# Attention with a squared-ReLU MLP on one core: the PV sums of a visit in a shared PSUM bank, copied by ScalarE and added up on GpSimd

## The chip, the cores and the metric

The kernel runs on one core of a Trainium2 chip. Its time is the device time of one execution in microseconds. All data are fp32; most matmuls read them as fp32r, and values that need more precision are split into a high and a low part that are multiplied apart.

## The reference

One layer norm feeds two branches. Branch A is attention with 32 heads of 16 columns over 2048 positions; branch B is a dense layer of 512 to 1792 with squared ReLU, a second dense layer back to 512, and SiLU. The output is `x + A * silu(B)`.

```python
xn = _layernorm(x)                                   # x: (1, 2048, 512)
q, k, v = split_heads(xn @ wqkv)                     # 32 heads of 16
p = softmax(einsum("bhqd,bhkd->bhqk", q, k) * 16 ** -0.5)
s = merge_heads(einsum("bhqk,bhkd->bhqd", p, v)) @ wo
h = relu(xn @ w1 + b1) ** 2                          # 512 -> 1792
g = silu(h @ w2 + b2)                                # 1792 -> 512
out = x + s * g
```

(`split_heads` and `merge_heads` stand for the reshapes and transposes of the reference.)

## The kernel before

**Units and steps.** Attention is cut into 32 units: four heads by 512 queries each. A unit has 16 steps, one for every 128 keys. A step has four matmuls of keys by queries, one a head, whose result goes through `exp` on ScalarE (`exp_mm`, matmul L1337, exp L1349), and the PV product of the four heads. In addition every step has four matmuls of queries by keys for a unit that is 24 steps ahead (`max_mm`, matmul L367); VectorE reduces each to the maximum over its 512 keys (L374). These maxima are the shift of the softmax: they come back into the query tiles as extra rows, so an exp needs no bias. We call the matmuls of L1337 and L367 the QK matmuls.

**Row tiles.** A QK matmul uses 64 rows of TensorE, so two matmuls run side by side in two lanes. The kernel fills the second lane with the dense layers of branch B, whose matmuls are cut into halves of 64 rows (L268 and L236). One round is what the two lanes start together: as a rule one QK matmul and one piece of dense work.

**Long slots.** `dense` yields the dense work in order, eight chunks of 256 positions. Where a piece has 12 units of work for each lane (`block`), `long_slots` spreads it over four steps: 28 rounds with 16 exps and 16 maxima. 24 rounds have dense work; the rounds in `DOUBLE` have a QK matmul in both lanes instead. The string in `ORDERS` says which QK matmul is an exp (`s`) and which a maximum (`m`). After 12, 16 and 28 rounds (`VISITS`) TensorE visits PV for 1, 1 and 2 steps. In the first dense layer a round has two matmuls of 256 columns, in the second one of 512. A chunk has 13 long slots; four of its steps, around the border between the two halves of its second layer, are single slots (`slot`), each with a PV visit of one step.

**PSUM.** There are eight banks. One (`pd`) holds the sums of the dense work. One (`pv`, tile `po`) holds the PV sums of a unit over all its 16 steps. Six hold results of QK matmuls: three are called `se`, three `pm_t`, but any of them may take an exp or a maximum. When the program is written out, a small model of TensorE's time picks the bank: `ROUND`, `FIRST_ROUND`, `STEP` and `VISIT` advance TensorE's clock, `READERS` and `READY` say when ScalarE or VectorE will have read a bank, and `flow_take` chooses one that is free by then. What happens on the chip is kept right by semaphores.

**PV.** `pv_mm` (L453) runs four matmuls, one a head, in four groups of 32 columns of TensorE, with `start` in the first step of a unit and `stop` in the last. After the last, `evac` copies the bank to the SBUF tile `ot` on ScalarE (L463). Then come, some steps apart, a DMA of the row sums (L473), their reciprocal on VectorE (L479), a DMA to DRAM and a broadcast back (L482, L488), the multiplication and a split on GpSimd (L502 to L504) and the stores (L511).

**The order of work.** TensorE, ScalarE, VectorE, GpSimd and SP's DMA queue each run their instructions in the order in which the program writes them. `later(n, fn)` writes `fn` out n steps later. GpSimd also squares and splits the first layer's result (L618, L109, L110) and adds the second layer's bias (L637), on which ScalarE's tanh waits (L642). Where one lane has finished its half of a dense block, a `fence` puts a `nop` on ScalarE that the other lane's first matmul waits for.

Three buffers `ex` in SBUF serve to load weights; that is over before unit 4.

Of the kernel before, what the change touches and what calls it, by code (L numbers as in the profile page):

```python
# [9 lines left out]
F32 = mybir.dt.float32  # L10
F32R = mybir.dt.float32r
AF = mybir.ActivationFunctionType
# [38 lines left out]
    [(0, 0), (0, 2), (1, 0), (1, 2), (2, 0), (2, 2)],  # L51
    [(0, 1), (0, 3), (1, 1), (1, 3), (2, 1), (2, 3)],
)
DOUBLE = (11, 13, 14, 27)
VISITS = {12: 1, 16: 1, 28: 2}
QUARTERS = (7, 14, 21, 28)
ORDERS = ("smsmsmsmsmssmmsmssmsmsmssmsmmmms", "smsmsmsmsmssmmsmssmsmsmssmsmmmms")
ROUND = 232
FIRST_ROUND = 335
STEP = 907  # L60
VISIT = 185
READY = 450
READERS = {"s": (476, 675), "m": (600, 745), "d": (600, 755)}
EPS = 1e-5


# [1 line left out]
def kernel(  # L68
# [56 lines left out]
    with ExitStack() as ph:  # L125
# [136 lines left out]
        def block(mms, per, post, between={}):  # L262


            def emit(ms, lane, follow):
                r = slice(64 * lane, 64 * lane + 64)
                for out_, lh, rh, first_, last_ in ms:
                    mm = nc.tensor.matmul(  # L268
                        out_, lh(r), rh(r),
                        start=first_ and lane == 0, stop=last_ and lane == 1,  # L270
                        skip_group_check=True,
                    )
# [12 lines left out]
            assert len(units) == 12  # L285
            yield [
                [
                    lambda m=m, lane=lane, k=k: [
                        emit(m, lane, None if k else last_use[0]),
                        lane and k in between and between[k](),  # L290
                    ][0]
                    for k, m in enumerate(units)
                ]
                for lane in range(2)
            ], post, ORDERS[per == 1]

        def terms3(ps, terms):

# [37 lines left out]
        def flow_visit(n):  # L336
            flow["pe"] += VISIT + n * STEP
            flow["fresh"] = True

        def flow_take(kind):  # L340
            free = [i for i, spot in enumerate(spots) if spot[0] <= flow["pe"] and spot[2] == kind]
            at, t, _ = spots.pop(min(free or range(len(spots)), key=lambda i: spots[i][0]))
            flow["pe"] = max(flow["pe"], at)
            return t

        def flow_give(t, kind):
            every, held = READERS[kind]
            begin_ = max(flow[kind], flow["pe"] + READY)
            flow[kind] = begin_ + every
            spots.append([begin_ + held, t, kind])  # L350

        def flow_bank(kind):
            t = flow_take(kind)
# [94 lines left out]
                        ),  # L448
                    )

        def pv_mm(po, qd, kb, pts):
            for j in range(4):
                nc.tensor.matmul(  # L453
                    po[32 * j : 32 * j + 32, :],
                    vs[qd][:, (4 * kb + j) * VW : (4 * kb + j) * VW + 32], pts[j],
                    start=(kb == 0), stop=(kb == NT - 1), skip_group_check=True,
                )

        def evac(po, u):
            qd, qc = divmod(u, 4)  # L460
            cs = slice(qc * 512, (qc + 1) * 512)
            ot = sp.tile([P, 512], F32, name="ot", bufs=1)
            nc.scalar.activation(ot, po, AF.Copy)  # L463
            if u == NU - 3:
                unit_mid(ot)
                return
            for n, fn in zip(EVAC, (evac_sums, evac_recip, evac_keep, evac_back, evac_norm, evac_store)):
                later(n, lambda fn=fn: fn(u, ev))
            ev = {"ot": ot}
# [1068 lines left out]
        def pv_step(st, pts):  # L1538
            u, kb = divmod(st, 16)
            if kb == 0:  # L1540
                pos[0] = pv.tile([P, 512], F32, name="po")
            pv_mm(pos[0], u // 4, kb, pts)
            if kb == NT - 1:
                if u < NU - 2:
                    evac(pos[0], u)
                elif u == NU - 2:
                    unit_inner(pos[0])
                else:
                    unit_final(pos[0])

        def dense():
            mp = ExitStack()
# [111 lines left out]
                post()  # L1664
            max_end(g)

        def long_slots(st0, units, post, order):

            if not spots:
                flow_start((pe, "se", "s", 3), (pm, "pm_t", "m", 3))  # L1670
            todo = [[(st0 + k, j) for k in range(4) for j in (lane, lane + 2)] for lane in range(2)]
            for kb in range(st0, st0 + 4):
                pts.setdefault(kb, {})
            ops, st, pv_at = list(order), st0, st0 - 2

            def fence(mm):
                use = nc.scalar.nop()
                tc.add_manual_dep(
                    use.ins, mm.ins.name,
                    mybir.DependencyInfo(  # L1680
                        mybir.DependencyClass.Sync, mybir.DependencyReason.DATA
                    ),
                    reason="the row tile is done with the bank",
                )
                last_use[0] = use

            def qk(lane):
                if ops.pop(0) == "m":
                    return max_mm(lane)
                kb, j = todo[lane].pop(0)  # L1690
                return exp_mm(kb, j, pts[kb], False)

            for r in range(len(order) - 4):
                if r in QUARTERS:
                    st += 1
                    begin(st)
                if r in DOUBLE:
                    for lane in range(2):
                        qk(lane)
                else:  # L1700
                    h = 0 if units[0] else 1
                    qk(1 - h)
                    mm = units[h].pop(0)()
                    if not units[h]:
                        if h and post is not None:
                            post()
                            last_use[0] = None
                        else:
                            fence(mm)
                flow_round()  # L1710
                if r + 1 in QUARTERS:
                    max_end(st + LEAD)
                    shift_due(st + 1 + LEAD)
                for _ in range(VISITS.get(r + 1, 0)):
                    pv_step(pv_at, pts.pop(pv_at))
                    pv_at += 1
                if r + 1 in VISITS:
                    flow_visit(VISITS[r + 1])
            assert not ops and not todo[0] and not todo[1] and not units[0] and not units[1]

        def plain_slot(st):
# [23 lines left out]
        for st_ in range(NU * 16):  # L1745
            if st_ < done:
                continue
            begin(st_)
            if st_ == FIRST:
                qs.close()  # L1750
            item = next(dn, None)
            if st_ == FIRST:

                for g in (LEAD, LEAD + 1):
                    max_end(g)
                for fn in last_store:
                    fn()
            if item is not None and len(item) > 2:
                assert st_ % 4 == 0
                long_slots(st_, *item)  # L1760
                done = st_ + 4
                to_visit[0] = st_ + 2
                continue
            wait = st_ >= LAST_MAX and item is not None and item[0] is not None and (st_ + flip[0]) % 2
            if item is not None and item[0] is not None:
                slot(st_, *item)
            else:

# [5 lines left out]
            for step in range(to_visit[0], st_ - 1):  # L1774
                pv_step(step, pts.pop(step))
            flow_visit(st_ - 1 - to_visit[0])
            to_visit[0] = st_ - 1
        assert not [1 for it in stream for _ in it] and not left
        run_waiting(True)
        assert not waiting and next(dn, None) is None  # L1780
        flow["on"] = False
        for st_ in range(to_visit[0], NU * 16):
            pv_step(st_, pts.pop(st_))
        wstk.close()


# [24 lines left out]
```

## Time and profile before

| What | us |
| --- | --- |
| median of three runs | 1616.87 |
| lowest and highest of the three | 1610.39 and 1617.13 |
| the profiled execution | 1610.35 |
| its span | 1608.6 |
| TensorE busy in the span | 1595.1 |
| VectorE busy | 1345.8 |
| ScalarE busy | 1189.6 |
| GpSimd busy | 534.9 |

In the rows of the profile PE is TensorE's matmuls, PEld its weight loads, DVE VectorE, ACT ScalarE and POOL GpSimd. A row of the timeline has the start in us from the start of the span, the duration in us, the engine, the line, the operation, the tiles written and read, their shapes, how many instructions are merged, and in brackets how long the engine sat idle before and what ended that. Matmuls overlap in the array and their ends are modelled, so the time between two starts says more than a duration. A row of a group has the sum and the mean (ns) of its instructions, then the idle time before them.

### The profile page before, as it was taken

To read this page: it belongs to the slowest core of one execution; us is meant where nothing else is said; L and a number is where in the kernel's file an instruction comes from. 1 tells how busy PE (TensorE), PEld (TensorE's weight loads), DVE (VectorE), ACT (ScalarE), POOL (GpSimd) and SP (SyncE) were. 2 spreads that over 40 slices of the span, in tenths; PEclk is the share of its full clock that TensorE was granted. 3 is DMA by queue.
4 is the path that set the end of the run, shared out by engine and by line. 5 is a ranking of instruction groups with operands and counts; after the bars stand their busy time and mean duration, and the time that the engine had idled before them with its cause. 6 is when DMAs were issued, how large, how long until landed. Compare 5 with 4: busy or idle time off the path is not lost.

```text
span 1608.6 us, 36225 instructions
## 1 busy us (share of the span) xinstructions
PE 1595.1 (99%) x13660; PEld 964.0 (60%) x13660; DVE 1345.8 (84%) x2307; ACT 1189.6 (74%) x2347; POOL 534.9 (33%) x610
## 2 busy tenths in 40 slices
PE   8999999999999999999999999999999999999998
PEld 7798665566546654665566456655665566545543
DVE  7486888888888888888888888888888888887764
ACT  7212777788778777887788778777877788778886
POOL 6436766233113311331133113311331134214621
PEclk9999999999999999999999999999999999999999
DMA  8977556435343433433434334433442253236755
GB/s 293 245 239 229 180 159 158 135 94 131 81 106 90 115 75 95 134 88 98 92 106 106 83 92 123 116 83 81 128 128 56 67 152 86 68 93 213 224 178 182
DMA packets 164174, 209.20 MB, mean 130 GB/s; under 512 B 59136, under 2 KB 79360, under 8 KB 162432
## 3 DMA queue, kind: packets, MB, share of 16 engines
q1 hardware_dynamic: 163856, 206.63, 46.4%
q8 instruction: 108, 1.77, 0.5%
q14 instruction: 66, 0.54, 0.1%
q10 hardware_dynamic: 144, 0.26, 0.0%
HBM read 148.90 MB, written 56.34 MB: 128 GB/s over the span
## 4 chain that ended last, share of the span: by engine, by line
PE 96%; DMA 1%; DVE 1%; issue 0%; SPq 0%; ACT 0%; POOL 0%; DVEq 0%
PE po L453 30%; PE pd_t L268 13%; PE pm_t L367 12%; PE se L1337 11%; PE se L367 8%; PE pm_t L1337 6%; PE pm_t L1206 4%; PE pd_t L236 4%; PE pm_t L236 2%; PE pd_t L1206 1%; PE se L1176 1%; PE se L1110 1%; PE pm_t L1297 0%; DVE mx L374 0%; PE se L236 0%
## 5 line engine op out<-in xcount | busy, mean ns | idle before, releaser
L374 DVE TENSOR_REDUCE mx<-pm_t 128x1 f32<-128x512 f32 x1236 | 799.2, 683 | 134.8 <-PE pd_t L268 82.4
L1349 ACT ACTIVATE pt<-se 128x512 f32<-128x512 f32 x1240 | 686.1, 606 | 182.8 <-PE pd_t L268 90.9
L374 DVE TENSOR_REDUCE mx<-se 128x1 f32<-128x512 f32 x795 | 528.5, 683 | 64.3 <-PE se L367 28.2
L1337 PE MATMUL se<-qe,ka 64*128 64x512 f32 x1346 | 530.4, 417 | 0.7 <-ACT pt L1349 0.7
L453 PE MATMUL po<-pt,v 128*32 128x512 f32 x3820 | 498.4, 602 | 0.2 <-DVE tsm L898 0.2
L367 PE MATMUL pm_t<-ka,qm 64*128 64x512 f32 x1236 | 480.4, 408 | 0.1
L1349 ACT ACTIVATE pt<-pm_t 128x512 f32<-128x512 f32 x666 | 388.9, 606 | 101.0 <-PE pd_t L268 58.5
L268 PE MATMUL pd_t<-xc,w1s 64*128 64x256 f32 x2352 | 328.8, 286 | 0.0
L1337 PEld LDWEIGHTS se<-qe,ka 64*128 64x128 f32 x1346 | 241.1, 184 | 137.1 <-ACT pt L1349 107.7
L367 PE MATMUL se<-ka,qm 64*128 64x512 f32 x795 | 310.6, 410 | 0.2
L268 PE MATMUL pd_t<-w2t,hT 64*128 64x512 f32 x1080 | 298.5, 408 | 0.0
L268 PEld LDWEIGHTS pd_t<-xc,w1s 64*128 64x128 f32 x2352 | 295.0, 186 | 0.0
L367 PEld LDWEIGHTS pm_t<-ka,qm 64*128 64x128 f32 x1236 | 222.9, 184 | 112.9 <-DVE mx L374 98.2
L1337 PE MATMUL pm_t<-qe,ka 64*128 64x512 f32 x695 | 283.6, 418 | 0.0
L453 PEld LDWEIGHTS po<-pt,v 128*32 128x32 f32 x3820 | 87.8, 108 | 158.7 <-issue 143.3
L268 PEld LDWEIGHTS pd_t<-w2t,hT 64*128 64x128 f32 x1080 | 180.9, 184 | 3.2
L367 PEld LDWEIGHTS se<-ka,qm 64*128 64x128 f32 x795 | 145.6, 184 | 51.5 <-DVE mx L374 36.0
L1337 PEld LDWEIGHTS pm_t<-qe,ka 64*128 64x128 f32 x695 | 126.3, 184 | 79.5 <-ACT pt L1349 64.4
L618 POOL TENSOR_TENSOR r<-r 128x512 f32<-128x512 f32 x56 | 58.2, 1039 | 321.1 <-ACT r L615 321.1
L502 POOL TENSOR_TENSOR ot<-ot,hl 128x512 f32<-128x512 f32 x27 | 34.7, 1286 | 154.5 <-DMA hl<-r_d 88.1
L637 POOL TENSOR_TENSOR u<-u,b_t 128x512 f32<-128x512 f32 x16 | 20.5, 1284 | 164.4 <-ACT u L636 164.4
L110 POOL TENSOR_TENSOR hT<-r,hT 128x512 fp32r<-128x512 f32 x56 | 72.5, 1295 | 4.7
(184 smaller groups left out, 1552.5 us busy)
## 6 DMA issues: line engine op xcount, KB each, us to landing
w1s<-w_d SPq DMA_DIRECT2D x196, 256.0 KB
qm<-q_d SPq DMA_DIRECT2D x384, 32.0 KB
ka<-k_d SPq DMA_DIRECT2D x96, 128.0 KB
qe<-q_d SPq DMA_DIRECT2D x384, 32.0 KB
q_d<-hl SPq DMA_DIRECT2D x16, 512.0 KB
g<-g_d SPq DMA_DIRECT2D x32, 256.0 KB
k_d<-hl SPq DMA_DIRECT2D x15, 512.0 KB
on_d<-hl SPq DMA_DIRECT2D x116, 64.0 KB
```

Of the source, the lines that this page charges most:

```text
L110: (lo or nc.gpsimd).tensor_tensor(dst[1], raw, dst[0].bitcast(F32), op=ALU.subtract)
L236: mm = nc.tensor.matmul(out_, lh(r), rh(r), start=first_ and lane == 0, stop=last_ and lane == 1, skip_group_check=True,)
L268: mm = nc.tensor.matmul(out_, lh(r), rh(r), start=first_ and lane == 0, stop=last_ and lane == 1, skip_group_check=True,)
L367: nc.tensor.matmul(ps, qms[u][p][64 * j : 64 * j + 64, qb * P : (qb + 1) * P], kas[qd, p][64 * j : 64 * j + 64, kc * 512 : (kc + 1) * 512] ...
L374: return nc.vector.tensor_reduce(mxs[u][:, c, kc : kc + 1], ps, axis=AX.X, op=ALU.max)
L453: nc.tensor.matmul(po[32 * j : 32 * j + 32, :], vs[qd][:, (4 * kb + j) * VW : (4 * kb + j) * VW + 32], pts[j], start=(kb == 0), stop=(kb = ...
L502: nc.gpsimd.tensor_tensor(ot, ot, rb, op=ALU.mult)
L618: nc.gpsimd.tensor_tensor(r, r, r, op=ALU.mult)
L637: nc.gpsimd.tensor_tensor(u, u, b2_t, op=ALU.add)
L1206: mm = nc.tensor.matmul(out_, lh(r), rh(r), start=first_ and lane == first, stop=last_ and lane != first, skip_group_check=True,)
L1337: nc.tensor.matmul(se, kas[qd, j // 2][b : b + 64, kb * P : (kb + 1) * P], qes[u][j // 2][b : b + 64, :], start=True, stop=True,)
L1349: return nc.scalar.activation(pts[j], se, AF.Exp, scale=0.25)
```

## The change

In units 4 to 27 a PV visit no longer adds to one bank over the whole unit. The bank `po` joins the six of the QK matmuls, seven in all, and each visit takes one of them, opens sums of its own in it and closes them at the visit's end. ScalarE copies them to SBUF: for the first visit of a unit into the unit's sum (`ot` in odd units, `ex0` in even ones), for the others into one of two part buffers (`ex1` and `ex2` in turn), which GpSimd adds to the sum. The steps after the last visit (`evac_chain`) are those of before, on that sum.

For long slots in these units the rounds with two QK matmuls move from 11, 13, 14 and 27 to 0, 13, 14 and 16, and there are two orders of exps and maxima, one for each dense layer. The numbers of the model that picks banks change for the whole kernel. In units 0 to 3 and 28 to 31 PV keeps its own bank.

```diff
-DOUBLE = (11, 13, 14, 27)
+DOUBLE = ((11, 13, 14, 27), (0, 13, 14, 16))
-ORDERS = ("smsmsmsmsmssmmsmssmsmsmssmsmmmms", "smsmsmsmsmssmmsmssmsmsmssmsmmmms")
+ORDERS = (
+    ("smsmsmsmsmssmmsmssmsmsmssmsmmmms",) * 2,
+    ("smmssmsmsmmssmmsmsssmsmmsssmsmmm", "msmsssmmssmsmmsmssmsmmsssmsmmmms"),
+)
+PARTS = range(4, 28)
-STEP = 907
-VISIT = 185
+STEP = 858
+VISIT = 226
-READERS = {"s": (476, 675), "m": (600, 745), "d": (600, 755)}
+READERS = {"s": (476, 785), "m": (600, 855), "d": (600, 865)}
+VISIT_READY = 160
...
         def flow_give(t, kind):
-            begin_ = max(flow[kind], flow["pe"] + READY)
+            begin_ = max(flow[kind], flow["pe"] + READY + (FIRST_ROUND - ROUND if flow["fresh"] else 0))
...
+        def flow_part(t):
+            begin_ = max(flow["s"], flow["pe"] + VISIT_READY)
+            flow["s"] = begin_ + READERS["s"][0]
+            spots.append([begin_ + READERS["s"][1], t, "s"])
...
-                    start=(kb == 0), stop=(kb == NT - 1), skip_group_check=True,
+                    start=first, stop=last, skip_group_check=True,
...
         def pv_step(st, pts):
             if kb == 0:
+                if u - 1 in PARTS:
+                    spots[:] = [spot for spot in spots if spot[1] is not pos["shared"]]
                 pos[0] = pv.tile([P, 512], F32, name="po")
-            pv_mm(pos[0], u // 4, kb, pts)
+            pv_mm(pos[0], u // 4, kb, pts, kb == 0, kb == NT - 1)
...
+        def pv_visit(st, n):
+            u, kb = divmod(st, 16)
+            if u not in PARTS:
+                for k in range(n):
+                    pv_step(st + k, pts.pop(st + k))
+                flow_visit(n)
+                return
+            if "shared" not in pos:
+                pos["shared"] = pv.tile([P, 512], F32, name="po")
+                spots.append([flow["pe"], pos["shared"], "s"])
+            po = flow_take("s")
+            for k in range(n):
+                pv_mm(po, u // 4, kb + k, pts.pop(st + k), k == 0, k == n - 1)
+            flow_visit(n)
+            if kb == 0:
+                if u % 2:
+                    pos["sum"] = sp.tile([P, 512], F32, name="ot", bufs=1)
+                else:
+                    pos["sum"] = rot["ex"][0]
+                nc.scalar.activation(pos["sum"], po, AF.Copy)
+            else:
+                rot["ex"][1:] = rot["ex"][:0:-1]
+                part = rot["ex"][1]
+                nc.scalar.activation(part, po, AF.Copy)
+                nc.gpsimd.tensor_tensor(pos["sum"], pos["sum"], part, op=ALU.add)
+            flow_part(po)
+            if kb + n == NT:
+                evac_chain(pos["sum"], u)
```

All places that ran `pv_step` over a visit's steps call `pv_visit` instead, and `long_slots` picks `DOUBLE` and `ORDERS` by whether its slot starts in one of these units.

More of the change, by code (lines that the diff above doesn't have):

```diff
@@ L294, in block @@
                 for lane in range(2)
-            ], post, ORDERS[per == 1]
+            ], post, per == 1
         def terms3(ps, terms):
@@ L449, in shift_rows, with pv_mm @@
                     )
-        def pv_mm(po, qd, kb, pts):
+        def pv_mm(po, qd, kb, pts, first, last):
             for j in range(4):
@@ L463, in evac, with evac_chain @@
             nc.scalar.activation(ot, po, AF.Copy)
+            evac_chain(ot, u)
+        def evac_chain(ot, u):
             if u == NU - 3:
@@ L1665, in slot, with long_slots @@
             max_end(g)
-        def long_slots(st0, units, post, order):
+        def long_slots(st0, units, post, second):
             if not spots:
@@ L1673, in long_slots @@
                 pts.setdefault(kb, {})
+            parts = st0 // 16 in PARTS
+            double, order = DOUBLE[parts], ORDERS[parts][second]
             ops, st, pv_at = list(order), st0, st0 - 2
@@ L1696, in long_slots @@
                     begin(st)
-                if r in DOUBLE:
+                if r in double:
                     for lane in range(2):
@@ L1713, in long_slots @@
                     shift_due(st + 1 + LEAD)
-                for _ in range(VISITS.get(r + 1, 0)):
-                    pv_step(pv_at, pts.pop(pv_at))
-                    pv_at += 1
                 if r + 1 in VISITS:
-                    flow_visit(VISITS[r + 1])
+                    pv_visit(pv_at, VISITS[r + 1])
+                    pv_at += VISITS[r + 1]
             assert not ops and not todo[0] and not todo[1] and not units[0] and not units[1]
@@ L1773 @@
                 continue
-            for step in range(to_visit[0], st_ - 1):
-                pv_step(step, pts.pop(step))
-            flow_visit(st_ - 1 - to_visit[0])
+            pv_visit(to_visit[0], st_ - 1 - to_visit[0])
             to_visit[0] = st_ - 1
@@ L1782 @@
         for st_ in range(to_visit[0], NU * 16):
-            pv_step(st_, pts.pop(st_))
+            pv_visit(st_, 1)
         wstk.close()
```

## Prediction

> **What bounds the kernel now.** I read the page's busy times first, then the timeline of TensorE over one long slot of each dense layer, then the weight loads that waited there, then ScalarE's and VectorE's own rows.
>
> ```profile
> PE 1595.1 (99%) x13660; PEld 964.0 (60%) x13660; DVE 1345.8 (84%) x2307; ACT 1189.6 (74%) x2347; POOL 534.9 (33%) x610
> 349.01:1435.22 1086.21, 1085.52 (x9589) 631.85 (x9589) 959.25 (x1609) 848.49 (x1684) 278.30 (x311) 1.00 0.39 99
> ```
>
> The second row is the window view from the evacuation of unit 3 to that of unit 27, 1086.2 us, where the change acts (columns: PE, PEld, DVE, ACT, POOL busy, clock, DMA). TensorE is busy throughout at full clock, so its small waits must be looked for inside the slots. A long slot is 28 rounds in segments of 12, 4 and 12, each followed by a PV visit. One whose dense work is the second layer, TensorE alone:
>
> ```profile
> 591.06 0.49 PE L1337 MATMUL pm_t<-qe,ka 64*128 64x512 f32 x1
> 591.39 0.39 PE L367 MATMUL se<-ka,qm 64*128 64x512 f32 x1
> ...
> 593.50 0.39 PE L1337 MATMUL se<-qe,ka 64*128 64x512 f32 x1
> ...
> 593.74 0.47 PE L1337 MATMUL pm_t<-qe,ka 64*128 64x512 f32 x1
> 593.76 0.49 PE L367 MATMUL pm_t<-ka,qm 64*128 64x512 f32 x1
> 594.18 1.07 PE L453 MATMUL po<-pt,v 128*32 128x512 f32 x8
> 595.18 0.50 PE L367 MATMUL se<-ka,qm 64*128 64x512 f32 x1
> ...
> 595.99 0.39 PE L367 MATMUL pm_t<-ka,qm 64*128 64x512 f32 x1
> 596.30 1.07 PE L453 MATMUL po<-pt,v 128*32 128x512 f32 x8
> 597.30 0.49 PE L1337 MATMUL se<-qe,ka 64*128 64x512 f32 x1
> ...
> 600.43 1.06 PE L453 MATMUL po<-pt,v 128*32 128x512 f32 x8
> ```
>
> The first round takes 0.33 us, later ones 0.23; in the middle segment PV starts 0.31 after the last round (595.99 to 596.30). By these, 12 rounds without a wait need 0.33 + 10 x 0.23 + 0.31, about 2.96 us. The two long segments take 3.12 (591.06 to 594.18) and 3.13 (597.30 to 600.43); the middle one, 1.12, has nothing to give. So **a second-layer slot holds about 0.33 us of waiting**. The wait sits at the end of each long segment, where both lanes ask for a bank at once:
>
> ```profile
> 591.59 0.60 ACT L1349 ACTIVATE pt<-pm_t 128x512 f32<-128x512 f32 x1 [1.61 <-PE pd_t L268]
> 593.07 0.59 ACT L1349 ACTIVATE pt<-pm_t 128x512 f32<-128x512 f32 x1
> 593.55 1.09 ACT L1349 ACTIVATE pt<-se 128x512 f32<-128x512 f32 x2
> 592.43 1.28 DVE L374 TENSOR_REDUCE mx<-pm_t 128x1 f32<-128x512 f32 x2
> 593.16 0.18 PEld L367 LDWEIGHTS pm_t<-ka,qm 64*128 64x128 f32 x1 [0.19 <-DVE mx L374]
> 593.72 0.18 PEld L1337 LDWEIGHTS pm_t<-qe,ka 64*128 64x128 f32 x1 [0.26 <-ACT pt L1349]
> ```
>
> An exp starts 0.53 after the matmul of a first round (591.06 to 591.59). The load that waits for its bank runs 0.65 after the exp's start (593.07 to 593.72), or 0.73 after a maximum's (592.43 to 593.16). Exps follow at 0.48 (593.07, 593.55), maxima at 0.60 (1.28 less one duration of 0.68). Counting banks with these numbers, from the segment's first matmul at 0: six are free; exps give banks back at 1.18, 1.66, 2.14, 2.62, maxima at 1.5, 2.1, 2.7. The last round begins at 2.65 and would need thirteen; by 2.6 there are eleven. Its loads should therefore run at 2.62 and 2.70; they ran at 2.66 (593.72) and beside it, so the count describes the trace. A late load is not hidden behind the matmul before it, hence 0.42 from the last round to PV instead of 0.31.
>
> With the first dense layer each round has two matmuls of 256 columns, and that lane is slower:
>
> ```profile
> 557.19 0.50 PE L268 MATMUL pd_t<-xc,w1s 64*128 64x256 f32 x2
> 557.53 0.40 PE L268 MATMUL pd_t<-xc,w1s 64*128 64x256 f32 x2
> ...
> 559.69 0.40 PE L268 MATMUL pd_t<-xc,w1s 64*128 64x256 f32 x2
> ...
> 560.33 1.07 PE L453 MATMUL po<-pt,v 128*32 128x512 f32 x8
> ...
> 562.12 0.28 PE L268 MATMUL pd_t<-xc,w1s 64*128 64x256 f32 x1
> ...
> 562.46 1.06 PE L453 MATMUL po<-pt,v 128*32 128x512 f32 x8
> ```
>
> Nine rounds from 557.53 to 559.69 are 0.24 each; from a last round PV needs 0.34 (562.12 to 562.46). Without waits 0.34 + 10 x 0.24 + 0.34 = 3.08, measured 3.14: **only 0.06 a segment, 0.12 a slot**, can be had there.
>
> **The change part by part.** By the loops, slots that start in units 4 to 27 are 89 long ones (41 second layer, 48 first layer) and 28 single ones. They make about 89 x 3 + 28 = 295 visits.
>
> *Removed.* The bank waits: 41 x 0.33 + 48 x 0.12 = 13.5 + 5.8 = 19.3 us. And one more. Where a unit ends, its evacuation sits on ScalarE ahead of the next segment's exps:
>
> ```profile
> 801.67 0.49 PE L1337 MATMUL se<-qe,ka 64*128 64x512 f32 x1
> 801.85 0.60 ACT L463 ACTIVATE ot<-po 128x512 f32<-128x512 f32 x1
> 802.35 2.55 ACT L1349 ACTIVATE pt<-se 128x512 f32<-128x512 f32 x5
> 802.48 0.59 SPq L473 DMA_DIRECT2D sm<-ot  x1
> 804.94 1.92 PE L453 MATMUL po<-pt,v 128*32 128x512 f32 x16
> ```
>
> That segment takes 3.27 instead of 3.13; 24 x 0.14 = 3.4. All waits together: 22.7 us.
>
> *Added on ScalarE.* 295 - 24 = 271 copies. A copy starts 0.18 after TensorE's next round and the exp 0.50 after it (801.67, 801.85, 802.35). 271 x 0.5 = 136 us, so a second-layer slot has 16 x 0.48 + 3 x 0.5 = 9.2 us of ScalarE in about 10.9; VectorE has 16 x 0.60 = 9.6. Neither is full. What counts is when banks return. New order, 12 rounds, doubled round first, seven banks, one of them PV's until its copy: six free; the copy's bank is back at 0.18 + 0.65 = 0.83; exps start at 0.68, banks at 1.33, 1.81, 2.29, 2.77; maxima start at 0.53, banks at 1.26, 1.86, 2.46. Asked for: 9 by 1.72, 10 by 1.96, 12 by 2.42, 13 by 2.65, and PV's at 2.96. There are 9, 11, 12, 13 and 14. **Nobody waits, with 0.04 to 0.2 us to spare.** In the last segment two banks come back only at 0.4 to 0.5, when 4 have been asked for; the rest is the same. The middle segment asks for six and the next visit's.
>
> So small a margin isn't kept in 178 long segments. The lower bound is no wait at all; the upper bound is the old 0.16 a segment, which takes the whole gain in second-layer slots. I take 0.05, nearer to the count, which met the trace to 0.04: 178 x 0.05 = 8.9 us back. It includes ScalarE's fence, the nop in round 12 that now stands behind a copy (0.18 + 0.50 = 0.68) while round 15 needs it at 0.80.
>
> By the Trainium skill, page "ScalarE: Activation LUTs", section "What ACT_TABLE_LOAD costs", an ACTIVATE takes 186 ns + 0.833 ns an element and neighbours overlap by about 93 ns: 0.52 us for 512 columns, not the trace's 0.48. With 0.52 the twelfth bank would come at 2.39 for a round that begins at 2.42, and each long segment would wait about 0.06: 10.7 us back instead of 8.9.
>
> *Added on GpSimd.* 271 additions.
>
> ```profile
> L637 POOL TENSOR_TENSOR u<-u,b_t 128x512 f32<-128x512 f32 x16 | 20.5, 1284 | 164.4 <-ACT u L636 164.4
> L618 POOL TENSOR_TENSOR r<-r 128x512 f32<-128x512 f32 x56 | 58.2, 1039 | 321.1 <-ACT r L615 321.1
> L110 POOL TENSOR_TENSOR hT<-r,hT 128x512 fp32r<-128x512 f32 x56 | 72.5, 1295 | 4.7
> L109 POOL TENSOR_SCALAR hT<-r 128x512 fp32r<-128x512 f32 x56 | 34.7, 619 | 4.9
> ```
>
> 271 x 1.284 = 348 us; a first-layer slot has 3 x 1.28 + 1.04 + 0.62 + 1.30 = 6.8 us in 11.1. They are covered by the two part buffers: a copy waits only for the addition two visits before, 5 us or more earlier in the long slots. Where the cover fails shows already, with GpSimd late after the normalisation of a unit:
>
> ```profile
> 607.52 1.28 POOL L502 TENSOR_TENSOR ot<-ot,hl 128x512 f32<-128x512 f32 x1 [13.06 <-DMA w1s<-w_d]
> 610.84 1.29 POOL L637 TENSOR_TENSOR u<-u,b_t 128x512 f32<-128x512 f32 x1
> 612.16 0.63 ACT L642 ACTIVATE r<-u 128x512 f32<-128x512 f32 x1 [1.41 <-POOL u L637]
> 613.33 0.50 PE L1337 MATMUL se<-qe,ka 64*128 64x512 f32 x1 [0.53 <-ACT pt L1349]
> ```
>
> The tanh waited 1.41 us for GpSimd, the exps stood behind it, and TensorE lost 0.5 us outright. The seven chunks have two such tanhs each; additions now stand ahead of them. Bounds: nothing, and 14 x 0.5 = 7 us. I take 3.
>
> *Moved.* The DMA of the sums (L473) left 0.03 after its copy ended (802.45); now it waits for an addition, some 1.4 us more, once a unit, with Q loads behind it on SP. Their first use is several steps of 2.8 us away; were that cover gone, 24 x 1.4 = 34 us. I take 0. PV's matmuls and visits stay as many; the banks planned in units 0 to 3 and 28 to 31 change by the new constants, 0 within 2 us either way.
>
> *Sum.* 22.7 - 8.9 - 3 = 10.8 us. The profiled run took 1610.35 (span 1608.6), so 1599.5. The three runs had a median of 1616.87 with the lowest, 1610.39, like the profiled one; a median of the new kernel may lie up to 6 us over the sum. I say 1602.
>
> **The rivals.** *A, the waits only move.* Each segment now starts with a copy, which cost 0.14 at a unit's end with six banks; if the seventh bank gives back just that, 0.16 - 0.14 = 0.02 is left in each of 82 second-layer segments, nothing in first-layer ones, and GpSimd takes its 3: 1610.35 - 1.6 + 3, about 1612. For it: the thin margins. Against it: the count has the copy in it.
>
> *B, slower: GpSimd becomes the bound after a unit's end.* L502 waits for the DMA that brings the reciprocals, and three instructions (607.52 to 610.84, 3.3 us) follow before any addition. In such a slot GpSimd has 6.8 + 3.3 = 10.1 us plus that wait. From a wait of about 5 us on, the addition is not done when ScalarE wants its part buffer again, exps stop behind the copy and TensorE with them. If each of 24 units lost 1.41 us so, 34 us: 1610.35 - 10.8 + 34, about 1633. For it: the row at 612.16. Against it: GpSimd is only a third busy and L502 comes in one slot of four. The Trainium skill, page "PSUM — Partial Sum Buffer", section "Engine vs sequencer instructions", says the queues of ScalarE and GpSimd are strict FIFO; by that rule a late normalisation must hold the additions and then the copies. The trace agrees: exps stood 1.41 us behind that tanh.
>
> *C, no waits at all*, as the count has it: 1610.35 - 22.7, about 1588.
>
> *D, the change doesn't do what it says:* the planner picks banks by its own clock; if it takes PV's bank too early, PV waits and the visits grow by 0.1 each, 295 x 0.1 = 30 us, less the 22.7 gained: 1618.
>
> **How the numbers follow.** Forecast 0.50, C 0.15, A 0.18, B 0.10, D 0.07. About 0.5%, 8 us, is what a measurement of this kernel can tell from no change. Faster takes the forecast (less a tenth for a median that falls short) and C: 0.61; slower takes B and half of D with a little of A: 0.15; the same 0.24. The range goes from 1586, below C, to 1618, which takes in A and D: 1586 to 1618. The forecast's own range is 1594 to 1607.
>
> **What would show it.** Right: second-layer slots near 11.0 us from one two-step visit to the next, long segments of 12 rounds at 3.0; first-layer ones at 11.15; weight loads that wait for ScalarE or VectorE gone from the last rounds; ScalarE up by about 140 us and GpSimd by about 350. Wrong: PV's first weight load waiting for an exp (D); copies waiting for GpSimd (B); loads waiting in rounds 8 to 11 as before (A).

## The result and the profile after

The changed kernel took 1596.43 us (median of four runs, 1595.33 to 1598.10), the kernel before beside it 1613.73 (1610.39 to 1617.13). The ratio is 0.9894, 95% interval 0.9864 to 0.9924: about 17 us or 1.1% faster. The profiled execution took 1595.56 us, 14.8 less than that of before.

Busy times of the changed kernel (busy time, share of the span, instructions):

```profile
PE 1576.5 (99%) x13660; PEld 960.7 (60%) x13660; DVE 1343.4 (84%) x2307; ACT 1318.7 (83%) x2618; POOL 880.8 (55%) x881
```

The window from the first PV matmul of unit 4 to that of unit 28 in the changed kernel (its bounds, its length, then busy time and instructions of PE, PEld, VectorE, ScalarE and GpSimd, the granted clock, the DMA share and GB/s):

```profile
352.10:1421.29 1069.19, 1066.28 (x9578) 628.55 (x9576) 958.23 (x1611) 978.26 (x1956) 624.32 (x583) 1.00 0.39 100
```

The same window in the kernel before:

```profile
352.08:1438.31 1086.23, 1085.54 (x9579) 630.97 (x9577) 959.28 (x1609) 848.51 (x1683) 278.30 (x311) 1.00 0.39 98
```

ScalarE has 271 instructions more in the whole program (2618 against 2347) and GpSimd 271 (881 against 610). They cost 130 and 346 us of busy time, and the stretch got 17.0 us shorter. TensorE does the same work with the same visits. A second-layer slot of the changed kernel, on TensorE's timeline:

```profile
586.74 0.50 PE L377 MATMUL pm_t<-ka,qm 64*128 64x512 f32 x1
586.74 0.50 PE L1350 MATMUL se<-qe,ka 64*128 64x512 f32 x1
...
589.40 0.39 PE L377 MATMUL se<-ka,qm 64*128 64x512 f32 x1
...
589.73 1.06 PE L463 MATMUL pm_t<-pt,v 128*32 128x512 f32 x8
...
592.84 0.50 PE L1350 MATMUL se<-qe,ka 64*128 64x512 f32 x1
...
595.82 1.49 PE L463 MATMUL pm_t<-pt,v 128*32 128x512 f32 x12
```

Its first segment on VectorE, on ScalarE, and the weight load of its thirteenth matmul:

```profile
587.27 0.69 DVE L384 TENSOR_REDUCE mx<-pm_t 128x1 f32<-128x512 f32 x1 [0.37 <-PE se L1350]
588.48 0.68 DVE L384 TENSOR_REDUCE mx<-se 128x1 f32<-128x512 f32 x1
```

```profile
586.93 0.60 ACT L1590 ACTIVATE ex<-pm_t 128x512 f32<-128x512 f32 x1 [1.01 <-PE pm_t L463]
587.43 0.59 ACT L1362 ACTIVATE pt<-se 128x512 f32<-128x512 f32 x1
587.90 0.60 ACT L1362 ACTIVATE pt<-pm_t 128x512 f32<-128x512 f32 x1
```

```profile
589.21 0.18 PEld L377 LDWEIGHTS se<-ka,qm 64*128 64x128 f32 x1
```

The long segments last 2.99 (586.74 to 589.73) and 2.98 us (592.84 to 595.82) instead of 3.12 and 3.13. The copy starts 0.19 after the round, the first exp 0.50 after the copy, the first maximum at 0.53, as in the prediction's count. The thirteenth matmul's load runs at 2.47 (589.21), 0.73 after the third maximum; the count had said 2.46. The prediction had expected that no load waits for ScalarE in the last rounds any more. One still does, that of the twelfth matmul:

```profile
589.05 0.18 PEld L1350 LDWEIGHTS se<-qe,ka 64*128 64x128 f32 x1 [0.17 <-ACT pt L1362]
589.16 0.39 PE L1350 MATMUL se<-qe,ka 64*128 64x512 f32 x1
```

It runs 0.11 us ahead of its matmul, where a load in time runs 0.23 ahead, and still neither this matmul nor the next (589.16, 589.40) falls behind the pace of 0.23 to 0.24 a round. Over the profile the medians are 10.95 us for a second-layer slot (11.24 before) and 11.09 for a first-layer one (11.25).

### The profile page after: what moved, and what is told of

Read it like the earlier page. It is cut to its first block, busy times and chain, and to the rows that moved or that the text cites. A ratio compares the mean times of both kernels' runs of the same rounds, so it can differ in the third digit from the quotient of the medians.

```text
span 1593.7 us, 37022 instructions
## 1 busy us (share of the span) xinstructions
PE 1576.5 (99%) x13660; PEld 960.7 (60%) x13660; DVE 1343.4 (84%) x2307; ACT 1318.7 (83%) x2618; POOL 880.8 (55%) x881
## 4 chain that ended last, share of the span: by engine, by line
PE 94%; DMA 2%; DVE 1%; POOL 1%; issue 1%; SPq 1%; ACT 0%; DVEq 0%; POOLq 0%; ACTq 0%
PE pm_t L463 16%; PE pd_t L273 15%; PE po L463 13%; PE se L1350 12%; PE pm_t L377 9%; PE se L377 6%; PE pm_t L1350 5%; PE pm_t L1219 4%; PE pd_t L241 3%; PE po L377 2%; PE pm_t L241 1%; PE po L1350 1%; PE pd_t L1219 1%; PE se L1189 1%; PE se L1123 1%; DVE mx L384 1%
## 5 line engine op out<-in xcount | busy, mean ns | idle before, releaser
L384 DVE TENSOR_REDUCE mx<-pm_t 128x1 f32<-128x512 f32 x1078 | 705.2, 684 | 126.3 <-PE pm_t L377 67.4
L384 DVE TENSOR_REDUCE mx<-se 128x1 f32<-128x512 f32 x690 | 454.5, 682 | 39.2 <-PE se L377 18.3
L1362 ACT ACTIVATE pt<-pm_t 128x512 f32<-128x512 f32 x545 | 326.3, 624 | 18.6 <-PE pm_t L1350 10.2
L463 PE MATMUL pm_t<-pt,v 128*32 128x512 f32 x2232 | 283.4, 602 | 0.0
L1591 POOL TENSOR_TENSOR ot<-ot,ex 128x512 f32<-128x512 f32 x136 | 175.3, 1289 | 143.8 <-ACT ex L1590 138.8
L1591 POOL TENSOR_TENSOR ex<-ex,ex 128x512 f32<-128x512 f32 x135 | 174.0, 1289 | 136.8 <-ACT ex L1590 134.9
L1350 PE MATMUL pm_t<-qe,ka 64*128 64x512 f32 x574 | 216.1, 400 | 0.0
L463 PE MATMUL po<-pt,v 128*32 128x512 f32 x1460 | 198.0, 602 | 1.5 <-DVE mx L384 1.3
L384 DVE TENSOR_REDUCE mx<-po 128x1 f32<-128x512 f32 x263 | 179.4, 682 | 19.3 <-PE po L377 10.2
L1590 ACT ACTIVATE ex<-pm_t 128x512 f32<-128x512 f32 x195 | 117.7, 603 | 50.3 <-PE pm_t L463 47.5
```

The source lines that it names most:

```text
L384: return nc.vector.tensor_reduce(mxs[u][:, c, kc : kc + 1], ps, axis=AX.X, op=ALU.max)
L463: nc.tensor.matmul(po[32 * j : 32 * j + 32, :], vs[qd][:, (4 * kb + j) * VW : (4 * kb + j) * VW + 32], pts[j], start=first, stop=last, ski ...
L1350: nc.tensor.matmul(se, kas[qd, j // 2][b : b + 64, kb * P : (kb + 1) * P], qes[u][j // 2][b : b + 64, :], start=True, stop=True,)
L1362: return nc.scalar.activation(pts[j], se, AF.Exp, scale=0.25)
L1590: nc.scalar.activation(part, po, AF.Copy)
L1591: nc.gpsimd.tensor_tensor(pos["sum"], pos["sum"], part, op=ALU.add)
```

## The experiments

All times are medians; the ratio is against the kernel before on the same chip. The last two columns are the medians of the long slots in units 4 to 27, between the starts of two two-step visits.

| Kernel | us | ratio, 95% interval | second layer | first layer |
| --- | --- | --- | --- | --- |
| changed | 1596.4 | 0.9894 (0.9864 to 0.9924) | 10.95 | 11.09 |
| model alone | 1612.3 | 0.9992 (0.9977 to 1.0007) | 11.24 | 11.25 |
| orders alone | 1617.5 | 1.0020 (1.0009 to 1.0031) | 11.32 | 11.34 |
| shared bank, old order | 1613.4 | 0.9999 (0.9987 to 1.0012) | 11.23 | 11.25 |
| six banks shared | 1646.5 | 1.0195 (1.0174 to 1.0215) | 11.61 | 11.58 |
| old model | 1601.6 | 0.9925 (0.9910 to 0.9941) | 11.01 | 11.21 |
| no additions | 1594.5 | 0.9896 (0.9881 to 0.9911) | 10.95 | 11.09 |
| one part buffer | 1685.0 | 1.0460 (1.0439 to 1.0482) | 10.95 | 11.17 |
| copy twice | 1744.8 | 1.0825 (1.0807 to 1.0843) | 12.73 | 12.74 |
| add twice | 1665.6 | 1.0333 (1.0317 to 1.0348) | 10.95 | 11.13 |
| late tanh | 1593.6 | 0.9876 (0.9859 to 0.9893) | 10.96 | 11.09 |
| and an early load | 1591.8 | 0.9858 (0.9842 to 0.9874) | 10.95 | 11.09 |

**The parts alone.** *Model alone* is the kernel before with the new constants:

```diff
-STEP = 907
-VISIT = 185
-READERS = {"s": (476, 675), "m": (600, 745), "d": (600, 755)}
+STEP = 858
+VISIT = 226
+READERS = {"s": (476, 785), "m": (600, 855), "d": (600, 865)}
...
-            begin_ = max(flow[kind], flow["pe"] + READY)
+            begin_ = max(flow[kind], flow["pe"] + READY + (FIRST_ROUND - ROUND if flow["fresh"] else 0))
```

> The kernel before with only the new constants of the bank model (STEP, VISIT, READERS and the term for a fresh round). Bank theory (a wait falls where more banks are asked for than readers have given back): the same six banks and the same order, so second-layer slots stay at 11.24 us, first-layer slots at 11.25, the whole within 4 us of the kernel before. Rival, the model is what helps, since it now picks the bank that is really free: slots fall to about 10.95 and 11.09 and the whole by 15 us.

It did nothing that can be measured: 0.9992.

*Orders alone* is the changed kernel with PV in its own bank throughout:

```diff
-                if u - 1 in PARTS:
+                if False:
...
-            if u not in PARTS:
+            if True:
```

> The changed kernel with PV left in its own bank in all units: new orders, doubled rounds and constants, six QK banks, no copies, no additions. Bank theory, counted as in the prediction: with both readers started in round 0 the exps give banks back at 1.18, 1.66, 2.14, 2.62 and the maxima at 1.26, 1.86, 2.46, so 12 of the 13 banks are there in time for the last round of a long segment and the 13th about 0.06 us late; a second-layer slot at 11.05 to 11.12, a first-layer slot at 11.10 to 11.17, the segment after a unit's end still 0.14 longer, the whole about 1602 us, some 9 us below the kernel before. Rival, the order alone gives it all and the seventh bank nothing: 10.95 and 11.09, about 1595 or less, since no copies are paid.

*Shared bank, old order* keeps the old doubled rounds too:

```diff
-            parts = st0 // 16 in PARTS
+            parts = False
```

> The changed kernel with the old order and the old doubled rounds (11, 13, 14, 27) in units 4 to 27: seven banks, copies and additions. Bank theory: six free at the start, the copy's bank at 0.83, exps at 1.33, 1.81, 2.29, maxima, which start a round later, at 1.50, 2.10: 12 of 13 by the last round, the 13th at about 2.70 or 2.77, and a doubled round at the end asks for two at once; a second-layer slot at 11.05 to 11.2, a first-layer slot at 11.15 to 11.25, the whole 1600 to 1607. Rival, the seventh bank gives it all: 10.95 and 11.09, 1595.

Both expectations missed: each part should have brought about half, and neither brought anything; the orders alone cost 0.2%. The last round of a long segment shows why. Orders alone:

```profile
592.78 0.49 PE L377 MATMUL pm_t<-ka,qm 64*128 64x512 f32 x1
594.79 0.62 ACT L1362 ACTIVATE pt<-pm_t 128x512 f32<-128x512 f32 x1
595.27 0.18 PEld L1350 LDWEIGHTS pm_t<-qe,ka 64*128 64x128 f32 x1
595.31 0.47 PE L1350 MATMUL pm_t<-qe,ka 64*128 64x512 f32 x1
595.46 0.18 PEld L377 LDWEIGHTS pm_t<-ka,qm 64*128 64x128 f32 x1
595.62 0.39 PE L377 MATMUL pm_t<-ka,qm 64*128 64x512 f32 x1
595.94 0.64 PE L463 MATMUL po<-pt,v 128*32 128x512 f32 x4
```

Shared bank, old order:

```profile
590.68 0.50 PE L1350 MATMUL se<-qe,ka 64*128 64x512 f32 x1
590.88 0.60 ACT L1590 ACTIVATE ex<-po 128x512 f32<-128x512 f32 x1 [1.29 <-PE po L463]
591.45 1.89 DVE L384 TENSOR_REDUCE mx<-pm_t 128x1 f32<-128x512 f32 x3 [0.55 <-PE pm_t L377]
593.38 0.18 PEld L377 LDWEIGHTS pm_t<-ka,qm 64*128 64x128 f32 x1
593.81 0.64 PE L463 MATMUL se<-pt,v 128*32 128x512 f32 x4
```

The thirteenth load ran at 2.68 (592.78 to 595.46) with the orders alone and at 2.70 (590.68 to 593.38) with the shared bank alone, as in the kernel before (2.70 by the count; 2.71 is the median of its long segments). Where such a load waits, PV starts 0.43 to 0.48 after it, so the segment ends at about 3.13 or 3.16 in all three. The count explains both dates. With the old order the seventh bank comes at 0.83, but the copy pushes every exp back by 0.15, so that only three of them instead of four return a bank by 2.64: twelve banks either way, and the thirteenth is VectorE's third at 2.70. With the new order and six banks VectorE's third comes at 2.46, but the thirteenth is ScalarE's fourth at 2.62, measured 2.68. The twelfth is late there as well: it is that third maximum's, its load ran at 2.49 (595.27), 0.04 ahead of its matmul, and the last round began 0.31 after that one (595.31 to 595.62). Only with both does the thirteenth come at 2.46. A load that is not late would run at about 2.42 (0.23 ahead of its matmul at 2.65). In the changed kernel the thirteenth ran 0.05 later than that and the twelfth 0.12 later than its own date (589.05, where the matmul before it began at 588.93), and neither did harm; 0.25 later costs 0.15 of the segment. So the gain is a threshold, not a sum of two halves. My expectation had the dates nearly right and took the delay of a load for the delay of the segment; it is the load's date plus 0.43 to 0.48.

*Six banks shared*, the changed kernel with one bank taken out while PV shares:

```diff
+                    spots.append(pos["spare"])
...
+                pos["spare"] = spots.pop(next(i for i, spot in enumerate(spots) if spot[2] == "m"))
```

> The changed kernel with one of the seven shared banks taken out of use in units 4 to 27: new orders, copies and additions, but six banks for QK and PV together. Bank theory: one bank fewer in every count, so each of rounds 7 to 11 of a long segment waits for the next return, 0.15 to 0.25 us a segment, and PV too may wait; second-layer slots at 11.3 to 11.5, first-layer slots at 11.3 to 11.4, the whole 1615 to 1630, slower than the kernel before. Rival, the number of banks does not matter and the orders do: within 4 us of the changed kernel's 1595.6.

The slots are 11.6 us, above the expectation, and the number of banks matters as the theory says.

```profile
597.97 0.50 PE L377 MATMUL po<-ka,qm 64*128 64x512 f32 x1
600.08 1.12 ACT L1362 ACTIVATE pt<-pm_t 128x512 f32<-128x512 f32 x2
600.76 0.18 PEld L377 LDWEIGHTS pm_t<-ka,qm 64*128 64x128 f32 x1
601.20 0.64 PE L463 MATMUL se<-pt,v 128*32 128x512 f32 x4
```

Five free banks and eight returns make thirteen; the eighth is ScalarE's at 2.77 by the count. The load ran at 2.79 (600.76) and PV started 0.44 later. The total was 1646 against 1615 to 1630, since the middle segment, which I had left out, waits too (1.28 instead of 1.13 us).

*Old model*, the change with the old constants (the diff of *model alone* turned round):

> The changed kernel with the old constants of the bank model. Bank theory: with seven banks and the new orders the count leaves 0.04 to 0.2 us to spare, but only if each matmul is given the bank that really returns first; the old constants call a bank free 0.11 us too early, so some matmuls are sent to a bank that is still being read: second-layer slots 11.0 to 11.1, the whole 2 to 8 us over the changed kernel. Rival, the choice of banks is round robin in effect and the constants do nothing: within 1 us. It also tells whether the 2.2 us lost in unit 29 of the changed kernel come from the constants: with the old ones they would be gone.

5 us over the changed kernel (1601.6), in the expected band; the last segment of a first-layer slot takes 3.18 us instead of 3.06. The constants matter only where the margin is thin. The losses in unit 29 stayed (2.1 us), so they don't come from the constants.

**GpSimd and ScalarE.** *No additions* leaves out the sum over a unit's visits:

```diff
-                nc.gpsimd.tensor_tensor(pos["sum"], pos["sum"], part, op=ALU.add)
```

> The changed kernel without the 271 additions on GpSimd; left out is the sum over a unit's visits, so each unit's result holds the first visit alone. If the losses in the single slots (steps 269, 381 and 437 in the profile of the changed kernel, 1.2, 0.6 and 0.3 us) come from GpSimd being late with the bias on which the tanh waits, they shrink and the whole gains 1 to 3 us: 1592.5 to 1594.5; long slots stay at 10.95 and 11.09. If additions also hold up copies in long slots, those get shorter and the gain is over 5 us. If GpSimd is fully covered: no change.

The same time (0.9896) and the same median slots: the 271 additions cost nothing that can be measured. The loss in the single slots did not shrink; against the profile of before it is 5.0 us, with the additions 3.6. In the changed kernel it looks like this:

```profile
917.92 1.30 POOL L650 TENSOR_TENSOR u<-u,b_t 128x512 f32<-128x512 f32 x1
919.17 2.63 POOL L1591 TENSOR_TENSOR ex<-ex,ex 128x512 f32<-128x512 f32 x2
919.25 0.63 ACT L655 ACTIVATE r<-u 128x512 f32<-128x512 f32 x1 [0.72 <-POOL u L650]
920.42 0.49 PE L1350 MATMUL se<-qe,ka 64*128 64x512 f32 x1 [0.81 <-ACT pt L1362]
```

The bias (L650) is late because the normalisation of the unit is ahead of it; the additions stand behind it. Without the additions the tanh even waited 1.4 us, in two places. TensorE stood 1.50 and 1.44 us there, and shortly after, from 611.0 and from 925.0 on, the clock granted to it was 0.50 for 3.4 us:

```profile
609.61 0.50 PE L1350 MATMUL se<-qe,ka 64*128 64x512 f32 x1 [1.50 <-ACT pt L1362]
611.00:614.40 3.40, 3.40 (x20) 2.67 (x18) 1.69 (x3) 2.79 (x6) 0.14 (x1) 0.50 0.36 94
```

(The second row is a window as above; the clock is the third number from its end.) The profile of the changed kernel has no such stretch in units 4 to 27.

*One part buffer*, *copy twice* and *add twice*:

```diff
-                rot["ex"][1:] = rot["ex"][:0:-1]
```

> The changed kernel with one part buffer instead of two, so that a copy waits for the addition of the visit just before. Theory, the two buffers cover GpSimd's delay: in most visits the addition is done anyway (copy 0.6 and addition 1.3 us after a visit, the next visit's end at least 2.1 us later), but in the slot in which a unit is normalised GpSimd is 3 to 8 us late, so ScalarE stands 2 to 4 us once a unit: the whole 20 to 60 us longer, 1615 to 1655. Rival, GpSimd is never late enough to matter: within 3 us of 1595.6.

```diff
+                nc.scalar.activation(part, part, AF.Copy)
```

> The changed kernel with a second ScalarE instruction at each visit but a unit's first, a copy of the part buffer onto itself, which holds no bank: ScalarE has 0.5 us more a visit. Theory, ScalarE is close to full after the change (16 exps of 0.48, three copies of 0.5 and 0.8 for the two Relus make 10.0 of 11.09 us in a first-layer slot, 9.2 of 10.95 in a second-layer one): first-layer slots become ScalarE-bound at about 11.5, second-layer ones lose their 0.04 to 0.2 us of slack and go to 11.1 to 11.3, the whole 1615 to 1630. Rival, ScalarE has room for a second copy, since it is busy only 83% of the span: under 5 us.

```diff
+                nc.gpsimd.tensor_tensor(part, part, pos["sum"], op=ALU.add)
```

> The changed kernel with a second addition on GpSimd after each (its result goes into the part buffer and is never used), 271 x 1.29 = 350 us more, GpSimd busy 1230 of some 1600 us. Theory of the prediction's rival B: a first-layer slot then has 10.6 of 11.1 us and one with a normalisation 14, so from there the additions fall behind, both part buffers stay taken and ScalarE stands 2 to 5 us a unit: 1640 to 1700. Rival, the cover of two buffers is deep enough for twice the work: under 5 us.

One buffer costs 89 us, above the expected band; the waits of ScalarE in that kernel:

```profile
ACT ex L1589 <- POOL ot L1590: 33.1, 10, 5.1
ACT ex L1589 <- POOL ex L1590: 32.4, 12, 4.0
```

22 waits of 3 us on the mean, one in nearly each unit, and the median slots are nearly untouched (10.95, 11.17): a few slots pay for all. ScalarE's waits reach TensorE, and they are not the whole price. In units 4 to 27 TensorE stood 53 us, in 22 waits of over 0.8 us; and in 15 stretches of 3.4 or 6.8 us, 68 us together, its granted clock was 0.50. Each stretch began within 2 us of the end of such a wait; seven of the waits, of 1.0 to 2.2 us, had none. The first stretch, with its window in the last row:

```profile
386.94 0.79 PE L1350 MATMUL po<-qe,ka 64*128 64x512 f32 x1 [3.44 <-ACT ex L1589]
388.44 0.62 PE L1350 MATMUL pm_t<-qe,ka 64*128 64x512 f32 x1
388.87 0.62 PE L377 MATMUL pm_t<-ka,qm 64*128 64x512 f32 x1
385.39:392.22 6.83, 5.28 (x33) 3.72 (x37) 2.58 (x4) 4.38 (x9) 3.02 (x3) 0.50 0.33 99
```

A round took 0.43 us there (388.44 to 388.87) instead of 0.24. By these numbers I estimate that the lower clock cost about 30 us of the 89. Twice the additions cost 69 us in the same way: 40 waits of ScalarE, 65.3 us; 22 of TensorE, 38 us; and 12 stretches at a clock of 0.50, 41 us. So the prediction's rival B is a real mechanism, and the second part buffer is what keeps it away: without that the change would have been 4.6% slower.

The second copy cost 148 us where I had expected 20 to 35. It is dearer than the first: it waits for the first to end. In that kernel:

```profile
619.15 0.60 ACT L1590 ACTIVATE ex<-pm_t 128x512 f32<-128x512 f32 x1 [1.30 <-PE pm_t L463]
619.78 0.63 ACT L1591 ACTIVATE ex<-ex 128x512 f32<-128x512 f32 x1
620.32 0.58 ACT L1362 ACTIVATE pt<-se 128x512 f32<-128x512 f32 x1
```

From the copy to the next exp 1.17 us (619.15 to 620.32) instead of 0.50; three such pairs, 16 exps of 0.48 and the 1.30 of idle time make 12.5 us, near the 12.7 of a second-layer slot. The three pairs add 2.0 us, and the slots got 1.65 to 1.78 longer. My expectation had counted 1.1 to 1.7 us a slot of ScalarE's time as free, and that was the error. From the first PV of unit 4 to that of unit 28 this kernel has

```profile
351.62:1571.69 1220.07, 1157.78 (x9578) 633.78 (x9576) 975.34 (x1611) 1130.32 (x2227) 621.60 (x583) 1.00 0.33 87
```

and so 89.8 us of idle ScalarE (1220.07 less 1130.32), against 90.9 in the changed kernel (1069.19 less 978.26). Most of it is the wait for the two-step visits, as in the 1.30 above, and the added copies did not move into it. So the changed kernel has next to none of ScalarE's time to spare, although ScalarE is busy for only 83% of its span.

**A better version.** *Late tanh* has two edits:

```diff
-                    later(2, gate)
+                    later(3 if 0 < c and tt == 0 else 2, gate)
...
+            if u + 1 not in PARTS and kb + n == NT:
+                spots[:] = [spot for spot in spots if spot[1] is not pos["shared"]]
```

> The changed kernel with two edits: the tanh of the first half of a chunk is written one step later (three steps after its evacuation instead of two, chunks 1 to 7), and PV's old bank is taken out of the QK banks right after the last visit of unit 27 instead of at the first visit of unit 28. Theory: the 1.2, 0.6 and 0.3 us at steps 269, 381 and 437 are the tanh waiting for GpSimd, and the 1.2 us at step 448 is PV waiting for VectorE to read that bank: 2 to 3.5 us less, 1592 to 1593.5. Rival, these are waits that fall elsewhere when moved: within 1 us of the changed kernel.

> The kernel with the late tanh once more, beside the one above on the same chip: 1593.6 us, as before; it is the base of the comparison.

1593.6 and 1594.6 us, 0.9876 and 0.9872. The second edit did what it should. In the changed kernel PV's first matmul of unit 28 waited for VectorE to read the shared bank:

```profile
1421.29 1.07 PE L463 MATMUL po<-pt,v 128*32 128x512 f32 x8 [1.29 <-DVE mx L384]
```

That wait is gone. The first edit freed the single slots (they lost 3.6 us against the kernel before, now they gain 1.3) and cost the next long slots almost as much: from unit 4 to the end of unit 27 the two kernels differ by 0.4 us. So for the tanh the rival was nearly right. Both ratios lie inside the interval of the changed kernel, so the times alone do not show a gain.

*And an early load*, on top of both:

```diff
-                    if c < 3 and tt == (1, 0, 2)[c]:
+                    if c < 3 and tt == (1, 0, 1)[c]:
```

> The kernel with the late tanh and the bank handed back early, and one edit more: the third load of attention outputs for the output projection is asked for one tile (two steps) earlier. In the profiles so far TensorE waits for that load, oc from on_d at step 476, between 0.2 us (kernel before) and 3.4 us (new constants alone), 1.4 in the changed kernel and 1.7 with the late tanh. Theory: this wait is the main part of what differs from run to run and took back 1.2 us of the change's gain; asked for earlier it goes, 1 to 2 us less: about 1591.5, and runs closer together. Rival: the load is late because the DMA queue is full there, so an earlier request only pushes the others: within 1 us of the kernel with the late tanh.

TensorE's wait for that load, in the changed kernel and then with the new constants alone:

```profile
PE pm_t L241 <- DMA oc<-on_d: 1.4, 1, 1.4
```

```profile
PE pm_t L236 <- DMA oc<-on_d: 3.4, 1, 3.4
```

With the early load there is no such row, and the kernel took 1591.82 us (1591.27 to 1592.04 in four runs), ratio 0.9858: the lowest of all versions, though its interval overlaps that of the changed kernel. The kernel with the late tanh beside it ran from 1590.54 to 1596.19, and their intervals overlap, so the step between these two is not settled by the times; the closer runs and the vanished wait fit the expectation. The wait can cost more than itself: in the profiles with the new constants alone and with the late tanh the granted clock was 0.50 for 3.4 us right after it (from 1527.4 and from 1507.4), in that of the changed kernel it was not.

## Why the prediction was right

The time on record was 1602 us with 1594 to 1607 as the forecast's own range; measured 1596.4. The sum had 10.8 us of gain, the profile has 14.8. Point by point:

- *What bounds the kernel.* Right. The waits at the ends of the long segments were where the time was, and the count of banks gave their dates to within 0.06 us in five kernels (2.66, 2.68, 2.70, 2.79 and 2.47 measured; 2.62, 2.62, 2.70, 2.77 and 2.46 counted, for the kernel before, the orders alone, the shared bank alone, six banks and the changed kernel). The rows show one segment of each; over the long segments of all second-layer slots between two two-step visits, first and second of a slot, the median date of the last QK load is 2.71 and 2.71, 2.69 and 2.65, 2.71 and 2.70, 2.79 and 2.79, and 2.48 and 2.51. Two figures of the count were off. By its own terms a segment without waits is 2.94 us, not 2.96. And the smallest margin in the dates given is 0.13 (the twelfth bank at 2.29 for a round at 2.42), not 0.04; the load of that round, due 0.23 ahead, is 0.10 late by the count, and it was, without harm.
- *Removed, 22.7 us.* From the start of unit 4 to the end of unit 27 the profile gained 18.3 us, although the single slots there lost 3.6: the long slots gave 21.8.
- *Given back, 0.05 in each of 178 segments, 8.9 us.* Mis-sized: if the 22.7 is taken as right, 22.7 - 21.8 leaves 0.9, about 0.005 a segment. The margins held, since a load can run 0.12 later than usual without harm. This is the term that made the sum too small. By the Trainium skill, page "ScalarE: Activation LUTs", section "What ACT_TABLE_LOAD costs", I had estimated 0.52 us from exp to exp, which would have made the term 10.7; they followed each other at 0.47 to 0.48 us here (587.43 to 587.90), so the trace does not agree with the page.
- *Added on ScalarE.* The copies cost the long slots next to nothing, as forecast, but "neither is full" was too hopeful: the second copy showed that the rest of ScalarE's time, 90.9 us in that stretch, took up none of the added work.
- *GpSimd, 3 us.* That the size was right (3.6) is luck, since the cause was not: without the additions the loss stays. What makes the bias late in the rows above is the normalisation ahead of it; that ScalarE's copies beside the tanh take the rest, I only argue, since no run took them from the single slots alone.
- *Moved, 0; other units, 0 within 2.* At unit 28's first visit PV waited for the shared bank, 1.2 us; that wait I had not named. In unit 29 two DMA waits took 2.2 us more than in the profile of before: VectorE's reciprocal stood 1.61 us for the row sums, which held TensorE up by 0.95, and TensorE stood 1.2 us longer for the load at step 476 (0.2 to 3.4 from kernel to kernel). Why these two DMAs were later stays open. 21.8 - 3.6 - 1.2 - 2.2 = 14.8, that of the profile.
- *The rivals.* C (1588) was nearer for the long slots than the forecast, and the losses outside them made up the difference; that the total fell into the forecast's own range is luck to that extent, since without the 3.4 us of losses that the sum had not named (1.2 and 2.2) the profile would stand at 1592, below it. A, that the seventh bank gives back just what the copy takes, is exactly what happens with the old order. It was the new order that decided against A. B did not occur, but one buffer less brings it about. D did not occur: PV's matmuls start 0.33 after the last round (589.40 to 589.73), and in a segment without waits it was 0.31 before.
- *The median.* I had added 2.5 us because the runs of before lay over their profiled one; the changed kernel's median is only 0.9 over its profiled 1595.56.

## What to carry to other kernels

Where a producer fills a ring of buffers in bursts, count the buffers returned by the date of the last request, with the readers' own start, cadence and hold time; that count told the dates of five kernels to less than 0.1 us. Such a gain can be a threshold, as here: a buffer more and an earlier start of the slower reader each did nothing, and together took away nearly all the waiting. Before handing work to an idle engine, ask what stands ahead of it in that engine's order, and give it enough buffers to be late; and before calling an engine's idle time free, look where in the loop it lies. For GpSimd one buffer was the difference between 1% faster and 5% slower.

## What the runs showed that I had not expected

A weight load that waits costs less than its wait. PV follows a load in time after 0.55 us (0.23 ahead of its matmul, and 0.32 more), but one that waited after 0.43 to 0.48, so a bank 0.25 us late cost 0.15 of the segment, and one 0.05 to 0.12 late cost nothing. After waits of TensorE as short as 1.4 us the granted clock could fall to 0.50 for 3.4 us, in which a round took nearly twice as long; with one part buffer such stretches added up to 68 us. A ScalarE copy that reads what the instruction before it wrote pushed the following exp back by 1.17 us instead of 0.50. And one wait of TensorE for one DMA near the end differed from kernel to kernel by up to 3 us (0.2 in the profile of before, 3.4 with the new constants alone), as much as some of the differences that were to be explained.
